# A linear-attention and MLP kernel: the weight loads are issued from ScalarE's queue after named steps, and each chunk's four input loads get staggered priorities

## The chip, the cores and the metric

The kernel runs on one core of one Trainium2 chip. The metric is device time in microseconds of one execution, as the median over repeated runs; lower is better. Before the change it is 200.94 us (three runs, 200.44 to 201.19).

## The reference

For 4 batches and 8 heads (sequence 768, head size 48, all float32) the reference runs a recurrence with a decay, lays the heads side by side, and sends the result through an MLP with a leaky ReLU:

```python
state = zeros(B, H, D, D)
for t in range(S):
    cur = einsum('bhd,bhe->bhde', u[None] * kt, vt)
    y[:, :, t] = einsum('bhd,bhde->bhe', rt, state + cur)
    state = wt[:, :, :, None] * state + einsum('bhd,bhe->bhde', kt, vt)
x = y.transpose(0, 2, 1, 3).reshape(B * S, H * D)      # 3072 x 384
h = x @ w_in                                           # 384 x 2048
out = maximum(0.01 * h, h) @ w_out                     # 2048 x 384
```

## The kernel before

**Chunks.** The 4 x 768 tokens are cut into 24 chunks of 128 tokens (`NCH`, six for each batch). A chunk needs four inputs, w, k, r and v, each a DMA of 192 KB in 192-byte rows: 128 tokens times 8 heads make 1024 rows (lines 288 to 295). The weights come in eight DMAs of 768 KB: four quarters of `w_in` in rows of 2048 bytes (384 rows each) and four of `w_out` in rows of 1536 bytes (512 rows each). Each quarter is cast to bf16 in two halves, one on DVE and one on ACT (lines 255 to 270).

**A chunk's preparation**, in the order in which one step needs the other: Ln of w on ACT (line 310); a cumulative sum on PE (325); the sum `ci` on DVE (340); two Exp on ACT, `er` (347) and `ek` (353); `rk`, which is r times `er` (360) and k times `ek` (366), on DVE; transposes on PE (379) with copies out on DVE (387) and ACT (389); scores on PE (450); the mask `m` on DVE (471); the sums for the state on PE (461) and the state on DVE (483, 485); the output product on PE (497, 501). On the side, POOL casts v to `vb` (316) and multiplies `ru` (406, 410), DVE reduces it to `dg` (414), and POOL makes `vs` from v and `dg` (418). DVE adds `y` (512), PE transposes it (521), and ACT copies it to `xT` (527). From chunk 16 on, the transposes are DMAs (397, 533).

**The MLP.** For each chunk there are four up steps (line 553: 12 matmuls each, quarter q of `w_in`), each followed by a leaky ReLU on ACT into `g` (587), and four down steps (line 605: 4 matmuls each, quarter q of `w_out`), then a copy on DVE (616) and the output DMA (620).

**The order of the work.** Nothing is scheduled on the chip: each engine, and each DMA queue with it, runs its instructions in the order in which they were written. That order comes from a list scheduler in the kernel, `Plan` (`order()`, from line 35). Each step is added with an engine, a planned duration, its dependencies and a priority. In planned time, a free engine takes the ready step with the lowest priority number, and among equals the one added first. A DMA step holds its queue for its planned duration; its planned transfer (`wire`) then waits for all transfers that were issued earlier, whatever the queue, and its data count as landed 1.5 us after that. The steps are emitted by planned start. Chunk n has priority P0 = 10n for its main steps, P0 + 1 for the scores, masks and outputs, and P0 + 2 for POOL's side work; the leaky ReLU has 5, the output copy 3, and the up and down steps have 1000 and more. Planned times decide only this order; on the chip each instruction waits for its semaphores.

**Buffers.** A `Ring` hands out a fixed set of tiles in turn, and whoever takes a tile again must wait for all earlier users of it. The ring `in` has 11 tiles, shared by chunk inputs and weights. The takes go: chunk 0 tile 0, chunk 1 tile 1, the `w_in` quarters tiles 2 to 5, chunk 2 tile 6, chunk 3 tile 7, the `w_out` quarters tiles 8, 9, 10 and 0, chunk 4 tile 1, chunk 5 tile 2, chunk 6 tile 3, and so on. So chunk 4 waits for the last reader of chunk 1, and chunks 5 and 6 wait for the casts of `w_in` quarters 0 and 1. The loads of chunk n also wait for the cumulative sum of chunk n - 5 (`AHEAD`), and the Ln of chunk n waits for the first up step of chunk n - 4 (`LEAD`). The cumulative sums, the scores and the outputs of a chunk each have a single PSUM tile, so the chunks pass these steps in order.

**Before the change** all loads are issued on SyncE's queue (SP), with the `w_in` quarters at priority 14, between chunks 1 and 2, and the `w_out` quarters at 34, between chunks 3 and 4. Their casts carry the same priorities.

Of the kernel before, what the change touches and what calls it, by code (L numbers as in the profile page):

```python
# [115 lines left out]
def kernel(  # L116
# [11 lines left out]
    nc = tc.nc  # L128
# [10 lines left out]
    NQ = FF // 512  # L139
# [1 line left out]
    LEAD = 4  # L141
    AHEAD = 5

    WEIGHTS = [(2, 14)] * 4 + [(4, 34)] * 4
    blocks = [1] * NCH
    assert sum(blocks) == NCH

# [41 lines left out]
    with tc.manual_schedule():  # L189
# [26 lines left out]
        def step(eng, dur, fn, pri, reads=(), writes=(), deps=(), wire=None):  # L216

            d = list(deps)
            for x in writes:
                d += x.old  # L220
            i = plan.add(eng, dur, fn, d, pri, wire)
            for x in (*reads, *writes):
                x.steps.append(i)
            return i
# [4 lines left out]
        def act(n, src=180):  # L229
            return (src + n) / 1200.0 + 0.02  # L230
# [4 lines left out]
        win_s, wout_s = [], []  # L235
        JQ = NJ // NQ

        def weight_steps(q, which, pri):
            st = in_r.take()

            def load(st=st, q=q):
                if which == 0:
                    nc.sync.dma_start(
                        out=st.t[:].rearrange("p (t f) -> p t f", t=KT),
                        in_=w_in_v[:, :, q * 512 : (q + 1) * 512],
                    )
                else:
                    nc.sync.dma_start(
                        out=st.t[:].rearrange("p (t f) -> p t f", t=JQ),
                        in_=w_out_v[:, q * JQ : (q + 1) * JQ, :],  # L250
                    )

            ld = step("SP", 0.45, load, pri, writes=[st], wire=2.2)
            made = []
            for half, eng in ((0, "DVE"), (1, "ACT")):
                def cast(st=st, q=q, half=half, eng=eng):
                    if which == 0:
                        f0 = half * 256
                        o = w_in_b[:, :, q * 512 + f0 : q * 512 + f0 + 256]
                        i = st.t[:].rearrange("p (t f) -> p t f", t=KT)[:, :, f0 : f0 + 256]  # L260
                    else:
                        n = JQ // 2
                        o = w_out_b[:, q * JQ + half * n : q * JQ + (half + 1) * n, :]
                        i = st.t[:].rearrange("p (t f) -> p t f", t=JQ)[:, half * n : (half + 1) * n, :]
                    if eng == "DVE":
                        nc.vector.tensor_copy(out=o, in_=i)
                    else:
                        nc.scalar.copy(out=o, in_=i)
                d = 0.65 if eng == "DVE" else act(768, 224)
                made.append(step(eng, d, cast, pri, reads=[st], deps=[ld]))  # L270
            (win_s if which == 0 else wout_s).append(made)


        xt_steps, cums, lns = [], [], []
        prev = None
        for n in range(NCH):
            b, c = divmod(n, C)
            t0 = c * L
            P0 = n * 10
            for i, (before, pri) in enumerate(WEIGHTS):  # L280
                if n == before:
                    weight_steps(i % NQ, i // NQ, pri)
            first, last = c == 0, c == C - 1
            slot = in_r.take()
            wn, kn, rn, vn = (
                View(slot, slot.t[:, i * DM : (i + 1) * DM].rearrange("p (h d) -> p h d", h=H)) for i in range(4))
            lds = []
            for src, use in ((w, wn), (k, kn), (r, rn), (v, vn)):
                def load(src=src, use=use, b=b, t0=t0):
                    nc.sync.dma_start(  # L290
                        out=use.t, in_=src[b, :, t0 : t0 + L, :].rearrange("h p d -> p h d")
                    )
                lds.append(step(
                    "SP", 0.45, load, P0, writes=[slot], wire=0.97,
                    deps=[cums[n - AHEAD]] if n >= AHEAD else []))
            if n == 0:
                u_ld = step(
# [4 lines left out]
                    P0, wire=0.6,  # L302
# [8 lines left out]
                P0, reads=[wn], writes=[lw], deps=[wl],  # L311
# [12 lines left out]
            def cum(cp=cp, lw=lw, tot=(not first and a_pe)):  # L324
# [18 lines left out]
                P0, reads=[cp, lw], writes=[ci], deps=[s_cum, s_ln],  # L343
# [5 lines left out]
                P0, reads=[cp], writes=[er], deps=[s_cum, s_ci],  # L349
# [5 lines left out]
                P0, reads=[ci], writes=[ek], deps=[s_ci],  # L355
# [6 lines left out]
                P0, reads=[rn, er], writes=[rk], deps=[rl, s_er],  # L362
# [5 lines left out]
                P0, reads=[kn, ek], writes=[rk], deps=[kl, s_ek],  # L368
# [25 lines left out]
            else:  # L394
# [4 lines left out]
                    P0, reads=[rk], writes=[rkT], deps=[s_r, s_k], wire=1.75)]  # L399
# [78 lines left out]
            if not last:  # L478
                sx = sx_r.take()
                s_st = []  # L480
                def state(sx=sx, pp=pp, sb=sb):
# [7 lines left out]
                    deps=[s_pp] + ([] if sb is None else s_sb)))  # L489
# [4 lines left out]
            def intra(m=m, vb=vb, yp=yp, rkT=rkT, sb=sb):  # L494
# [13 lines left out]
                deps=s_m + s_T + [s_vb] + ([] if sb is None else s_sb))  # L508
# [69 lines left out]
        for rank, (kind, nb, item) in enumerate(seq):  # L578
            pri = 1000 + rank
            if kind == 0:  # L580
                up, j, J, N, g, m_chs, deps = item
                hp = hp_r.take()
                s_up = step("PE", J * 3 * (N / 2400 + 0.0025), lambda up=up, hp=hp: up(hp), pri,
                            writes=[hp], deps=deps)
# [13 lines left out]
            else:  # L598
                ch, q, g, off = item
# [8 lines left out]
                deps = [g_done[nb, j] for j in range(q * NJ // 4, (q + 1) * NJ // 4)]  # L608
# [50 lines left out]
```

## Time and profile before

| | before |
|---|---|
| median of the runs | 200.94 us |
| the profiled execution | 199.18 us |
| its span, first to last instruction | 197.4 us |
| busy: PE, DVE, ACT, POOL | 175.4, 134.9, 113.7, 101.8 us |
| bytes moved on the one DMA queue of the kernel | 32.97 MB |

The profile is one execution. "Busy" counts the time in which an engine executes; for PE it is modelled, since matmuls overlap, so a busy PE is not always a PE at full rate. A row such as `29.60 1.53 SPq L290 ...` in a timeline gives start and duration of an instruction in microseconds from the start of the span, then its engine (SPq is SyncE's sequencer, which issues DMAs) and line. In the DMA view, the last number of a row is the median time from issue to landing.

### The profile page before, as it was taken

Reading aid. Unit: us, or ns where it says so; the run is one execution under the profiler, and the core shown is the slowest. Engines: PE = TensorE matmul, PEld = TensorE weight load, DVE = VectorE, ACT = ScalarE, POOL = GpSimd, SP = SyncE. Lnnn points to the kernel's source line nnn. Section 1 sums busy time; section 2 is a strip of 40 time slices with the busy share of each in tenths; the row PEclk is TensorE's granted clock in tenths of the full one; section 3 lists DMA queues with packets and bytes.
Section 4 is the critical chain, followed back from the end, with each engine's and each line's share of the span. In section 5 each row is a group of like instructions: output and inputs, shape, how many; then the busy total and the mean of one; then the engine's idle time right before and its main releaser. Section 6 shows DMA issues by size and latency. Waiting matters only on the chain.

```text
span 197.4 us, 5816 instructions
## 1 busy us (share of the span) xinstructions
PE 175.4 (89%) x2360; PEld 137.7 (70%) x2360; DVE 134.9 (68%) x223; ACT 113.7 (58%) x249; POOL 101.8 (52%) x126
## 2 busy tenths in 40 slices
PE   0426884999999999999999999999999989999992
PEld 0315773678777878767877788777778768778870
DVE  6578459856998989699988989647876665441111
ACT  3434795557785865846576765656565546434430
POOL 2483068245888997898698796571813110100000
PEclk9999998599999999999999999999999999999999
DMA  6999999989999999989999968989735729422002
GB/s 122 200 285 378 179 203 382 286 167 195 186 191 189 196 216 183 241 171 223 182 227 193 221 145 145 210 159 184 118 90 113 49 68 116 95 64 59 29 15 79
DMA packets 118954, 33.34 MB, mean 169 GB/s; under 512 B 112144, under 2 KB 117392, under 8 KB 118928
## 3 DMA queue, kind: packets, MB, share of 16 engines
q1 hardware_dynamic: 118928, 32.97, 82.6%
q8 instruction: 18, 0.29, 0.7%
q14 instruction: 8, 0.07, 0.1%
HBM read 25.36 MB, written 4.72 MB: 152 GB/s over the span
## 4 chain that ended last, share of the span: by engine, by line
PE 73%; DMA 8%; DVE 7%; ACT 5%; SPq 2%; issue 2%; POOL 1%; DVEq 0%; POOLq 0%
PE op L605 29%; PE hp L553 29%; PE sc L450 3%; PE sc L379 3%; DMA in<-in_r_dram 3%; DMA rkT<-rk 3%; DMA in<-in_v_dram 2%; PE yp L501 2%; SPq L290 2%; PE yp L461 2%; DVE m L471 2%; PE cp L325 2%; PE yp L497 1%; DVE rk L366 1%; DVE rk L360 1%
## 5 line engine op out<-in xcount | busy, mean ns | idle before, releaser
L587 ACT ACTIVATE g<-hp 128x512 bf16<-128x512 f32 x96 | 57.2, 598 | 47.7 <-PE hp L553 47.1
L553 PE MATMUL hp<-xT,w_in_b 128*128 128x128 bf16 x1152 | 81.8, 223 | 1.3 <-ACT xT L527 0.9
L553 PEld LDWEIGHTS <-w_in_b 128*128 128x128 bf16 x1152 | 71.9, 100 | 10.2 <-issue 1.0
L605 PE MATMUL op<-w_out_b,g 128*128 128x384 bf16 x384 | 78.3, 330 | 0.0
L605 PEld LDWEIGHTS <-g 128*128 128x128 bf16 x384 | 33.4, 98 | 14.2 <-issue 0.7
L406 POOL TENSOR_TENSOR ru<-in,ub 128x384 f32<-128x384 f32 x24 | 24.9, 1039 | 19.4 <-DMA in<-in_r_dram 18.6
L439 POOL TENSOR_TENSOR sb<-s,a 128x384 bf16<-128x384 f32 x20 | 19.6, 978 | 26.1 <-ACT a L432 16.6
L471 DVE TENSOR_TENSOR m<-sc,maskb 128x1024 bf16<-128x1024 f32 x24 | 29.2, 1219 | 5.3 <-PE sc L450 4.6
L616 DVE COPY o<-op 128x384 f32<-128x384 f32 x24 | 13.3, 552 | 18.3 <-PE op L605 18.3
L410 POOL TENSOR_TENSOR ru<-ru,in 128x384 f32<-128x384 f32 x24 | 25.4, 1056 | 0.4
L418 POOL TENSOR_TENSOR vs<-in,dg 128x384 f32<-128x384 f32 x24 | 20.7, 866 | 8.4 <-DVE dg L414 5.5
L366 DVE TENSOR_TENSOR rk<-in,ek 128x384 bf16<-128x384 f32 x24 | 20.5, 853 | 0.9 <-ACT ek L353 0.8
L360 DVE TENSOR_TENSOR rk<-in,er 128x384 bf16<-128x384 f32 x24 | 16.8, 701 | 5.4 <-ACT er L347 5.2
L340 DVE TENSOR_TENSOR ci<-cp,lw 128x384 f32<-128x384 f32 x24 | 13.2, 550 | 7.4 <-ACT g L587 4.0
L316 POOL CAST vb<-in 128x384 bf16<-128x384 f32 x24 | 13.2, 552 | 9.4 <-DMA in<-in_v_dram 7.2
L512 DVE TENSOR_TENSOR y<-yp,vs 128x384 bf16<-128x384 f32 x24 | 13.2, 550 | 7.0 <-PE yp L501 5.8
L347 ACT ACTIVATE er<-cp 128x384 f32<-128x384 f32 x24 | 11.9, 497 | 10.2 <-DVE ci L340 10.2
L379 PE MATMUL sc<-ident,rk 128*128 128x128 bf16 x128 | 13.2, 235 | 4.8 <-DVE rk L360 2.9
L389 ACT COPY rkT<-sc 128x512 bf16<-128x512 bf16 x16 | 9.4, 586 | 12.7 <-PE sc L379 6.7
L414 DVE TENSOR_REDUCE dg<-ru 128x8 f32<-128x384 f32 x24 | 13.0, 543 | 3.7 <-POOL ru L410 3.6
L379 PEld LDWEIGHTS <-rk 128*128 128x128 bf16 x128 | 8.8, 103 | 7.6 <-DVE rk L360 4.0
L310 ACT ACTIVATE lw<-in 128x384 bf16<-128x384 f32 x24 | 12.5, 520 | 2.1 <-DMA in<-in_w_dram 1.8
(39 smaller groups left out, 149.3 us busy)
## 6 DMA issues: line engine op xcount, KB each, us to landing
in<-in_w_dram SPq DMA_DIRECT2D x24, 192.0 KB, 4.3
in<-in_k_dram SPq DMA_DIRECT2D x24, 192.0 KB, 4.3
in<-in_r_dram SPq DMA_DIRECT2D x24, 192.0 KB, 4.8
in<-in_v_dram SPq DMA_DIRECT2D x24, 192.0 KB, 4.3
out_dram<-o SPq DMA_DIRECT2D x24, 192.0 KB, 2.6
in<-in_moe_w_in_dram SPq DMA_DIRECT2D x4, 768.0 KB, 7.9
in<-in_moe_w_out_dram SPq DMA_DIRECT2D x4, 768.0 KB, 8.3
ub<-in_u_dram SPq DMA_DIRECT2D x1, 192.0 KB, 4.6
```

What stands on the lines that cost most here:

```text
L360: lambda rk=rk, rn=rn, er=er: nc.vector.tensor_tensor(out=rk.t[:, 0, :, 0:D], in0=rn.t, in1=er.t[:], op=ALU.mult),
L366: lambda rk=rk, kn=kn, ek=ek: nc.vector.tensor_tensor(out=rk.t[:, 1, :, 0:D], in0=kn.t, in1=ek.t[:], op=ALU.mult),
L379: nc.tensor.transpose(trv[:, a, g, :], rk.t[:, a, 2 * g : 2 * g + 2, :].rearrange("p h d -> p (h d)"), ident[:])
L406: lambda ru=ru, rn=rn: nc.gpsimd.tensor_tensor(out=ru.t[:], in0=rn.t, in1=ubv, op=ALU.mult),
L410: lambda ru=ru, kn=kn: nc.gpsimd.tensor_tensor(out=ru.t[:], in0=ru.t[:], in1=kn.t, op=ALU.mult),
L418: lambda vs=vs, vn=vn, dg=dg: nc.gpsimd.tensor_tensor(out=vs.t[:], in0=vn.t, in1=dg.t[:].unsqueeze(2).to_broadcast([128, H, D]), op=ALU.mult),
L439: lambda sb=sb, s_in=s_in, a_in=a_in: nc.gpsimd.tensor_tensor(out=sb.t[:].rearrange("p g a d -> p (g a) d"), in0=s_in.t[:].rearrange("p g ...
L471: lambda m=m, sc=sc: nc.vector.tensor_tensor(out=m.t[:].rearrange("p a g t -> p (a g) t"), in0=sc.t[:].rearrange("p a g t -> p (a g) t"), ...
L553: nc.tensor.matmul(hp.t[:, a * N : (a + 1) * N], lhsT=w_in_b[:, t, (j + a) * 128 : (j + a + 1) * 128], rhs=xT[:, t, c0 : c0 + N], start=(a ...
L587: lambda hp=hp, g=g, j=j, J=J, N=N: nc.scalar.activation(out=g.t[:, j : j + J, 0:N], in_=hp.t[:, 0 : J * N].rearrange("p (a n) -> p a n", ...
L605: nc.tensor.matmul(op.t[:], lhsT=g.t[:, j, off : off + 128], rhs=w_out_b[:, j, :], start=(j == 0), stop=(j == NJ - 1))
L616: "DVE", dve(DM, 120), lambda o=o, op=op: nc.vector.tensor_copy(out=o.t[:], in_=op.t[:]),
```

## The change

The eight weight loads move from SyncE's queue to ScalarE's. Each now depends on one Ln step, chunk 0's for `w_in` and chunk 2's for `w_out` (the third number of each `WEIGHTS` entry), and the priorities of loads and casts go from 14 to 2 and from 34 to 3. The planner is told 0.1 us on ACT for an issue in place of 0.45 us on SP, a transfer of 2.0 us in place of 2.2, and 0.95 in place of 0.97 for an input load. The four input loads of a chunk get priorities P0, P0 + 0.1, P0 + 0.2 and P0 + 0.3; the load of `u`, which was added after them, keeps P0 of chunk 0.

```diff
-    WEIGHTS = [(2, 14)] * 4 + [(4, 34)] * 4
+    WEIGHTS = [(2, 2, 0)] * 4 + [(4, 3, 2)] * 4
...
-        def weight_steps(q, which, pri):
+        def weight_steps(q, which, pri, after):
...
-                    nc.sync.dma_start(
+                    nc.scalar.dma_start(
                         out=st.t[:].rearrange("p (t f) -> p t f", t=KT),
                         in_=w_in_v[:, :, q * 512 : (q + 1) * 512],
                     )
                 else:
-                    nc.sync.dma_start(
+                    nc.scalar.dma_start(
                         out=st.t[:].rearrange("p (t f) -> p t f", t=JQ),
                         in_=w_out_v[:, q * JQ : (q + 1) * JQ, :],
                     )
 
-            ld = step("SP", 0.45, load, pri, writes=[st], wire=2.2)
+            ld = step("ACT", 0.1, load, pri, writes=[st], deps=[lns[after]], wire=2.0)
...
-            for i, (before, pri) in enumerate(WEIGHTS):
+            for i, (before, pri, after) in enumerate(WEIGHTS):
                 if n == before:
-                    weight_steps(i % NQ, i // NQ, pri)
+                    weight_steps(i % NQ, i // NQ, pri, after)
...
-            for src, use in ((w, wn), (k, kn), (r, rn), (v, vn)):
+            for i, (src, use) in enumerate(((w, wn), (k, kn), (r, rn), (v, vn))):
...
                 lds.append(step(
-                    "SP", 0.45, load, P0, writes=[slot], wire=0.97,
+                    "SP", 0.45, load, P0 + 0.1 * i, writes=[slot], wire=0.95,
                     deps=[cums[n - AHEAD]] if n >= AHEAD else []))
```

## The prediction

> **What bounds the kernel now.** I read the page first: the busy shares, then the slices.
>
> ```profile
> span 197.4 us, 5816 instructions
> ...
> PE   0426884999999999999999999999999989999992
> ...
> PEclk9999998599999999999999999999999999999999
> DMA  6999999989999999989999968989735729422002
> GB/s 122 200 285 378 179 203 382 286 167 195 186 191 189 196 216 183 241 171 223 182 227 193 221 145 145 210 159 184 118 90 113 49 68 116 95 64 59 29 15 79
> ```
>
> A slice is 4.9 us. From slice 7 (35 us, the slices counted from 0) PE is full to the end; before it there are holes, and slices 6 and 7 have a lower granted clock. The DMA engines are full from slice 1 to about slice 20, at some 190 GB/s, and at 380 GB/s where weights pass. So the first 35 to 40 us are a DMA stage, and everything after them is a queue of PE work. Next I read the windows, over all engines, then for the down and the up matmuls alone.
>
> ```profile
> 15.00:20.00 5.00, 3.43 (x34) 2.79 (x35) 4.36 (x7) 2.15 (x3) 1.37 (x2) 1.00 1.03 377
> 35.00:40.00 5.00, 5.00 (x37) 3.13 (x36) 4.24 (x8) 2.53 (x4) 1.07 (x1) 0.52 1.04 264
> 60.00:65.00 5.00, 4.93 (x76) 4.10 (x75) 4.43 (x8) 3.05 (x9) 4.45 (x7) 1.00 0.94 208
> 53.00:193.70 140.70, 139.15 (x1935) 109.63 (x1931) 97.81 (x161) 83.53 (x187) 76.17 (x88) 1.00 0.78 147
> ...
> 0.00:53.00 53.00, 10.09 (x44) 4.21 (x44) 0.94 1.01 235
> ...
> 0.00:53.00 53.00, 14.52 (x187) 13.18 (x188) 0.94 1.01 235
> ```
>
> From 53.0 to PE's last work at 193.7 us PE idles 140.70 - 139.15 = 1.55 us. So the span is set by how much matmul work is done by some early time, say 53 us, when before has done 44 down matmuls (first short row) and 187 up matmuls (last row). Their rates, at full clock, are in the chain of waits, with two pieces of a chunk's preparation:
>
> ```profile
> 40.17 0.65 PE op L605 x4
> ...
> 45.56 0.67 PE hp L553 x12
> ...
> 65.86 0.22 PE sc L379 x4
> ...
> 67.57 0.33 PE sc L450 x8
> ```
>
> A down matmul is 0.65 / 4 = 0.163 us, an up matmul 0.67 / 12 = 0.056 us.
>
> **Part 1: the order on SP changes by more than the weights that leave it.** This decides my forecast, and it comes out of the planner's rules with the code's own costs, worked by hand (an order is taken from them, no time). In the changed plan, chunk 0's w lands at 0.45 + 0.95 + 1.5 = 2.9, its Ln is done at 3.5, and the `w_in` issues follow at once on ACT. Eight input or `u` transfers are queued ahead of them (to 7.70), so quarters 0 and 1 land at 11.2 and 13.2; v of chunk 1, issued between quarters 1 and 2, lands at 14.15. The casts now have priority 2 instead of 14, so they pass chunk 1's steps: quarter 0 is cast by 12.7 and quarter 1 by 14.1. That frees tiles 2 and 3, which are those of chunks 5 and 6. Tile 1, for chunk 4, waits for chunk 1's `vs`, which needs that v and a `dg` at about 15.0: done at about 15.9. So SP is given chunks 2, 3, **5, 6, 4**. In the old plan `vs` and the late cast come at 15.2 and 15.5, and chunk 4 goes first. My margins are 3.2 us for chunk 5 and 1.8 for chunk 6, against an error by hand of perhaps 1.
>
> The `w_out` issues wait for chunk 2's Ln, at about 21 in the plan. By then the transfers of chunks 2, 3, 5, 6 and 4 are queued (to 35.65), so the plan has `w_out` landing from 39.15, but chunk 4's w at 34.3 and r at 36.2. So Ln, cumulative sum, Exp and the transposes of chunk 4 are written ahead of the `w_out` casts on ACT and DVE, and ahead of the first down step on PE. Whatever the chip does with `w_out`, no down matmul starts until chunk 4's r has landed and been worked on.
>
> **Part 2: when that is.** SP's timeline, and four answers of the DMA view for the issues at 29.60, 40.55, 44.22 and 46.32:
>
> ```profile
> 26.47 3.04 SPq L248 DMA_DIRECT2D in<-in_moe_w_out_dram  x4
> 29.60 1.53 SPq L290 DMA_DIRECT2D in<-in_w_dram  x1
> ...
> 40.55 0.73 SPq L290 DMA_DIRECT2D in<-in_w_dram  x1
> ...
> 44.22 1.06 SPq L290 DMA_DIRECT2D in<-in_w_dram  x1
> ...
> 46.32 0.98 SPq L290 DMA_DIRECT2D in<-in_r_dram  x1
> ```
> ```profile
> in<-in_w_dram SPq DMA_DIRECT2D x1, 192.0 KB, 11.2
> ...
> in<-in_w_dram SPq DMA_DIRECT2D x1, 192.0 KB, 4.1
> ...
> in<-in_w_dram SPq DMA_DIRECT2D x1, 192.0 KB, 4.5
> ...
> in<-in_r_dram SPq DMA_DIRECT2D x1, 192.0 KB, 5.0
> ```
>
> The w of chunks 4, 5 and 6 lands at 40.8, 44.7 and 48.7, one load a microsecond. In the new order chunk 4 comes where chunk 6 is now: w at 48.7, r at 46.32 + 5.0 = 51.3. That holds if the engines' total work ahead of it is unchanged, in whatever order the queues share it: the DMA share is 0.94 where only inputs pass and 1.03 where only weights do, so there is no free room for one beside the other. The Trainium skill, "DMA: Bandwidth & Descriptors", section "Issuing engines are not separate DMA queues", speaks against the change in the same sense: DMAs from SyncE and ScalarE interleave on the same 16 engines, and a second issuer saves issue time only. Both shares agree with it.
>
> From r on the path goes over DVE: `rk`, twice, then the copy of the transposes and the first cast. The groups:
>
> ```profile
> L366 DVE TENSOR_TENSOR rk<-in,ek 128x384 bf16<-128x384 f32 x24 | 20.5, 853 | 0.9 <-ACT ek L353 0.8
> ...
> L360 DVE TENSOR_TENSOR rk<-in,er 128x384 bf16<-128x384 f32 x24 | 16.8, 701 | 5.4 <-ACT er L347 5.2
> ```
> ```profile
> 35.07 1.44 PE L605 MATMUL op<-w_out_b,g 128*128 128x384 bf16 x4
> ```
>
> 51.3 + 0.70 + 0.85 makes 52.85, and the first down step comes at about 53, where it starts at 35.07 now. Bounds: 51.3 if the cast needs nothing behind r, and 54.5 if it stands behind chunk 4's `dg`. I take 53, as the `w_out` step becomes ready in the plan between the two.
>
> **Part 3: the sum.** At 53 us the changed kernel has done all 192 up matmuls of chunks 0 to 3 and no down matmul. It lacks 44 x 0.163 = 7.2 us, has 5 x 0.056 = 0.3 us more, and is behind by part of a chunk's preparation: with eight transposes (2 x 0.22), eight scores (0.33) and as much again for the rest, a chunk takes about 1.6 us; half of one, 0.8 us. Together 7.7 us. PE has little to do before 53 us, so it may restart at a low clock: the row at 35.00 shows 0.52 over 5 us, a loss of 2.4 us, which before has already paid within its 53 us. Between 0 and 2.4 I take 1.2. Of the 1.55 us of later idling, waits for inputs should go, since PE comes later than they do: 0 to 1.55 back, I take 1.0. The sum is 7.7 + 1.2 - 1.0 = **+7.9 us**: 207.1 us against the profiled execution's own 199.18 (197.4 of span and 1.8 around it), and 208.8 us against the median of 200.94.
>
> **Part 4: what is hidden.** The `u` load overtakes k, r and v of chunk 0, since it keeps P0 and they no longer do; it holds SP 0.93 us. And the four `w_in` issues stand on ACT between chunk 0's Ln and `er`:
>
> ```profile
> 3.54 0.93 SPq L299 DMA_DIRECT2D ub<-in_u_dram  x1
> ...
> 8.67 3.10 SPq L243 DMA_DIRECT2D in<-in_moe_w_in_dram  x4
> ...
> 3.93 0.52 ACT L310 ACTIVATE lw<-in 128x384 bf16<-128x384 f32 x1 [1.85 <-DMA in<-in_w_dram]
> 5.61 0.49 ACT L347 ACTIVATE er<-cp 128x384 f32<-128x384 f32 x1 [1.16 <-DVE ci L340]
> ```
>
> No DMA is issued on ACT now. Four issues took SP 3.10 us; ACT may take between nothing and that. From 4.45 the issues end at 7.55 at most, so `er` moves by up to 1.9 us, beside the wait for r. The other four (3.04 us on SP) block ACT after chunk 2's Ln, with copies of transposes and leaky ReLUs behind them; the fourth also waits for the readers of chunk 0, long done. I cost both at nothing, as the down steps wait for chunk 4 until 53 anyway; without that cover they cost 2 to 5 us. The 6.1 us that SP no longer spends on weights give nothing back: its issues are held up by the full queue (0.7 to 1.5 us each above).
>
> **The rivals.** *The queues add up (faster).* If the 190 GB/s is a limit of SP's queue and not of the engines, weights pass beside inputs. The weights take about 17 us of the shared line (8 x 0.79 MB at 377 GB/s), so chunk 4's w lands at 48.7 - 17 = 31.7, 9 us sooner than now. PE's holes in slices 3 to 6 come to 4.9 x (0.4 + 0.2 + 0.2 + 0.6) = 6.9 us and the low clock to 2.4; of these 9 us some 6 would be filled: 195 us. It decides from where chunk 4's w lands by about 41, as it does now. For it: 190 against 380 GB/s. Against: both shares at 1. Chance 0.13. *The order of the chunks stays 4, 5, 6.* If my hand plan errs by over 2 us, chunk 4 lands as now, the weights a few us sooner, and PE fills part of the same holes with down steps, until it runs out of chunks: some 2 us, 199 us, chance 0.12. *It does nothing:* the same bytes, the same PE work, gains and losses cancel within half a percent (1.0 us, about what can be told from no change here); 201 us, chance 0.07. *Weights crowd out the first chunks (slower still).* If the engines alternate row by row between the queues, four `w_in` quarters (4 x 384 rows) let only 1536 input rows pass, 1.5 loads, over some 10 us from about 6.5. Chunk 0's v then lands near 14, chunk 1's w near 17; in the plan chunk 1's Ln stands on ACT ahead of a copy of chunk 0 (7.3 against 7.8), so everything up to the first up step moves to about 21.6, and chunk 3's up steps (4 x 0.67 = 2.7 us) slip behind 53: 211.6 us, chance 0.18. The first up step shows today at:
>
> ```profile
> 18.60 1.46 PE L553 MATMUL hp<-xT,w_in_b 128*128 128x128 bf16 x12 [0.39 <-DVE w_in_b L266]
> ```
>
> The Trainium skill's same page, "Queues, rings and completion order", says that each engine goes round its queues packet by packet, which is this rival's mechanism; with one queue in use, no run here shows it yet.
>
> **How the numbers follow.** My forecast has 0.50: 208.8, with 205 to 212 of its own from the bounds (first down step 51.3 to 54.5, clock 0 to 2.4, idling 0 to 1.55). Slower by over 0.5% are the forecast and the crowding, 0.68; within 0.5% the last but one, 0.07; faster the first two rivals, 0.25. The range runs from 197.5, which leaves out the queues that add up (0.13), to 214, which leaves out the end of the crowding.
>
> **What would show it.** Right: SP's chunk loads in the order 2, 3, 5, 6, 4; chunk 4's w landing near 48 and r near 51; the first down step on line 605 near 53, with `w_out` landed well before; PE in holes until then and full after. A DMA share near 1 and a sum of rates no better than 380 GB/s while both queues are active. Wrong: chunk 4's loads ahead of 5 and 6, a first down step before 45, or 192-byte loads landing at one a microsecond while weights pass.

## The result and the profile after

The changed kernel takes 220.46 us (three runs, 219.96 to 222.07) against 200.94 before: 1.0995 times as long, with a 95% interval of 1.09 to 1.1089. Some executions of a kernel run slower than the rest, and a ratio with an interval is taken over the fast ones alone, so it need not be the quotient of the two medians. The forecast was 208.8 with a range up to 214. The direction was right; of the 19.5 us that were lost, the forecast had 7.9.

The page of the changed kernel, span and slices (5.5 us each):

```profile
span 218.3 us, 5803 instructions
...
PE   0004872085998999999999999999999999999993
...
PEclk9999969655599999999999999999999999999998
DMA  5999999999994399894794687599894432521111
GB/s 124 327 266 257 187 172 250 293 288 188 179 192 63 93 187 214 184 194 94 130 181 96 125 146 156 102 201 176 154 162 104 103 89 48 123 57 54 39 38 72
```

PE does next to nothing in the first three slices, and in slices 6 and 7 (33 to 44 us) it has a hole that the kernel before does not have. It is full from slice 10 (55 us), not from 35 us. The DMA engines are full up to slice 11 and then short of work for two slices; they were never slack while PE waited. The granted clock is low in slice 5 and in slices 7 to 10, ahead of the hole, in it and behind it.

Next the windows with all engines: the changed kernel from 65.5 us to PE's last work, then the same for the kernel before.

```profile
65.50:214.30 148.80, 147.18 (x2003) 114.58 (x2000) 105.94 (x168) 88.92 (x197) 78.17 (x89) 1.00 0.61 123
```
```profile
65.50:193.70 128.20, 126.71 (x1756) 99.68 (x1753) 86.03 (x142) 74.63 (x168) 65.37 (x76) 1.00 0.75 142
```

From 65.5 us on PE is full in both: 1.62 and 1.49 us idle. The changed kernel simply has 147.18 - 126.71 = 20.5 us more PE work left at that moment, and its span is 20.9 us longer. So the loss lies wholly ahead of 65.5 us. For the down matmuls (line 605) alone, then the up matmuls (553), the same view of the changed kernel has:

```profile
0.00:65.50 65.50, 0.00 (x0) 0.02 (x1) 0.82 1.10 227
...
0.00:65.50 65.50, 17.48 (x192) 16.08 (x192) 0.82 1.10 227
```

This is the state that the prediction foresaw, 192 up and no down matmuls, but 12.5 us later than the 53 us it gave. PE's timeline shows the two places (start, duration, and in brackets the idle time ahead and who ended it):

```profile
23.94 1.44 PE L553 MATMUL hp<-xT,w_in_b 128*128 128x128 bf16 x12 [0.57 <-ACT xT L527]
...
44.22 2.72 PE L553 MATMUL hp<-xT,w_in_b 128*128 128x128 bf16 x24 [9.84 <-ACT g L587]
...
65.53 1.46 PE L605 MATMUL op<-w_out_b,g 128*128 128x384 bf16 x8
```

The first up step comes at 23.9 us (before, 18.6), and PE then waits 9.84 us for a leaky ReLU of ScalarE. ScalarE's timeline says why:

```profile
3.71 11.61 ACTq L243 DMA_DIRECT2D in<-in_moe_w_in_dram  x4
...
15.37 0.49 ACT L347 ACTIVATE er<-cp 128x384 f32<-128x384 f32 x1 [11.15 <-DMA in<-in_v_dram]
...
32.75 10.78 ACTq L248 DMA_DIRECT2D in<-in_moe_w_out_dram  x4
...
43.57 0.60 ACT L587 ACTIVATE g<-hp 128x512 bf16<-128x512 f32 x1 [10.23 <-DMA in<-in_v_dram]
```

ScalarE stands still twice, 11.6 and 10.8 us, while it issues four DMAs each time, and the timeline puts both waits down to the landing of a chunk's v. Neither `er` nor `g` reads a v. Seen in narrower windows, the issues themselves are short; the third and the fourth of each set are late:

```profile
6.62 0.44 ACTq L243 DMA_DIRECT2D in<-in_moe_w_in_dram  x1
...
14.95 0.38 ACTq L243 DMA_DIRECT2D in<-in_moe_w_in_dram  x1
...
40.15 0.37 ACTq L248 DMA_DIRECT2D in<-in_moe_w_out_dram  x1
...
43.15 0.38 ACTq L248 DMA_DIRECT2D in<-in_moe_w_out_dram  x1
```

And the chain that ended last has these pieces, the two DMA rows being its longest of all:

```profile
3.02 11.91 DMA in<-in_v_dram
14.93 0.02 issue
14.95 0.38 ACTq L243
...
33.78 9.27 DMA in<-in_v_dram
43.07 0.04 ACTq L248
43.11 0.04 issue
43.15 0.38 ACTq L248
```

The fourth `w_in` issue starts at 14.95, when v of chunk 0 has landed (3.02 + 11.91 = 14.93); the fourth `w_out` issue at 43.15, when v of chunk 6 has (43.05). These are loads of SyncE, into other tiles. The compiled program has the link: every DMA of SyncE and of ScalarE signals one of eight semaphores, dealt in turn in the order in which the DMAs stand in the program, and waits, before it is issued, for the last DMA that had its semaphore, which is the eighth before it. Eight before the fourth `w_in` load stands v of chunk 0; eight before the fourth `w_out` load, v of chunk 6. The third issues agree: eight before them stand k of chunk 0 and k of chunk 6, which were issued at 1.92 and 32.18 and landed 4.7 and 7.9 us later, and the third issues start at 6.62 and 40.15. As long as SyncE issued everything, only SyncE waited there. On ScalarE the same wait holds up whatever is written behind it: Exps, leaky ReLUs, copies. DMAs of GpSimd have semaphores of their own and carry no such wait.

### The profile page after: what moved, and what is told of

It is laid out like the page before. It is cut to its first block, busy times and chain, and to the rows that moved or that the text cites. A ratio compares the mean times of both kernels' runs of the same rounds, so it can differ in the third digit from the quotient of the medians.

```text
span 218.3 us, 5803 instructions
## 1 busy us (share of the span) xinstructions
PE 178.2 (82%) x2360; PEld 141.0 (65%) x2360; DVE 136.9 (63%) x223; ACT 114.6 (52%) x249; POOL 102.0 (47%) x126
## 4 chain that ended last, share of the span: by engine, by line
PE 63%; DMA 14%; DVE 11%; issue 5%; ACT 3%; SPq 2%; ACTq 0%; DVEq 0%
PE hp L553 26%; PE op L605 23%; DMA in<-in_v_dram 10%; DMA rkT<-rk 5%; PE sc L379 4%; PE sc L450 3%; DVE m L471 2%; DVE rk L360 2%; PE yp L461 2%; DVE rkT L387 1%; SPq L290 1%; PE yp L501 1%; ACT rkT L389 1%; PE cp L325 1%; DVE rk L366 1%
## 5 line engine op out<-in xcount | busy, mean ns | idle before, releaser
L553 PE MATMUL hp<-xT,w_in_b 128*128 128x128 bf16 x1152 | 84.4, 227 | 11.4 <-ACT g L587 9.8
L553 PEld LDWEIGHTS <-w_in_b 128*128 128x128 bf16 x1152 | 74.2, 102 | 18.8 <-issue 10.5
L605 PE MATMUL op<-w_out_b,g 128*128 128x384 bf16 x384 | 77.0, 326 | 1.0 <-DVE w_out_b L266 1.0
L439 POOL TENSOR_TENSOR sb<-s,a 128x384 bf16<-128x384 f32 x20 | 18.2, 910 | 28.2 <-ACT a L432 20.8
L410 POOL TENSOR_TENSOR ru<-ru,in 128x384 f32<-128x384 f32 x24 | 26.1, 1087 | 0.4
L379 PE MATMUL sc<-ident,rk 128*128 128x128 bf16 x128 | 13.5, 241 | 13.8 <-DVE rk L360 12.6
L316 POOL CAST vb<-in 128x384 bf16<-128x384 f32 x24 | 14.4, 601 | 6.9 <-DMA in<-in_v_dram 6.9
L310 ACT ACTIVATE lw<-in 128x384 bf16<-128x384 f32 x24 | 12.4, 518 | 1.7 <-DMA in<-in_w_dram 1.6
```

The lines of the kernel that those rows point to most:

```text
L316: lambda vb=vb, vn=vn: nc.gpsimd.tensor_copy(out=vb.t[:], in_=vn.t),
L379: nc.tensor.transpose(trv[:, a, g, :], rk.t[:, a, 2 * g : 2 * g + 2, :].rearrange("p h d -> p (h d)"), ident[:])
L410: lambda ru=ru, kn=kn: nc.gpsimd.tensor_tensor(out=ru.t[:], in0=ru.t[:], in1=kn.t, op=ALU.mult),
L439: lambda sb=sb, s_in=s_in, a_in=a_in: nc.gpsimd.tensor_tensor(out=sb.t[:].rearrange("p g a d -> p (g a) d"), in0=s_in.t[:].rearrange("p g ...
L553: nc.tensor.matmul(hp.t[:, a * N : (a + 1) * N], lhsT=w_in_b[:, t, (j + a) * 128 : (j + a + 1) * 128], rhs=xT[:, t, c0 : c0 + N], start=(a ...
L605: nc.tensor.matmul(op.t[:], lhsT=g.t[:, j, off : off + 128], rhs=w_out_b[:, j, :], start=(j == 0), stop=(j == NJ - 1))
```

## The experiments

The theory: the loss has three parts, the planned order (as all on one queue would show it), the crowding of the chunk inputs by weights on a second queue, and ScalarE's second stop. Rivals: the late chunk 4 alone, the crowding alone, or the first stop. Where nothing else is said a time is one run, beside a run of the kernel before at 199.3 to 201.0. Seventeen runs of the kernel before spread from 198.05 to 202.31; of their pairs one in six differs by over 2 us and one in seventeen by over 3 us, so a difference under 3 us between two single runs is not taken for one. The versions are explained one by one below; "act" in a name is ScalarE. "Stops" are the stretches from the first to the last of ScalarE's four `w_in` and four `w_out` issues, in us.

| version | us | first up step | first down step | stops |
|---|---|---|---|---|
| after | 220.46 | 23.94 | 65.53 | 11.6, 10.8 |
| win_act_wout_gpsimd | 209.61 | 23.98 | 54.88 | 11.7, none |
| win_gpsimd_wout_act | 220.69 | 24.46 | 66.28 | none, 12.4 |
| same_plan_on_gpsimd | 209.81 | 23.57 | 55.33 | none |
| same_plan_on_sync | 204.96 | 15.73 | 46.87 | none |
| only_win_on_act | 209.86 | 24.38 | 55.45 | 12.1, none |
| only_wout_on_act | 210.46 | 15.45 | 55.80 | none, 3.4 |
| fewer_dmas | 216.72 | 22.75 | 61.89 | 0.4, none |
| win_at_start | 216.56 | 28.74 | 52.83 | 9.6, 11.8 |
| chunks_in_order | 214.32 | 23.78 | 54.15 | 11.5, 6.3 |
| four_first | 221.79 | 24.03 | 67.18 | 11.7, 12.3 |
| four_first_gpsimd | 209.38 | 23.18 | 54.36 | none |
| four_first_sync | 203.12 | 15.61 | 47.23 | none |

**Each stop taken away by itself.** Each of these two moves one set of weights to GpSimd's queue, so that both sets still pass on another queue than the inputs, with the same plan.

```diff
 # win_act_wout_gpsimd: only the w_out issue
-                    nc.scalar.dma_start(
+                    nc.gpsimd.dma_start(
                         out=st.t[:].rearrange("p (t f) -> p t f", t=JQ),
```

> The changed kernel with one edit: the w_out quarters are issued on GpSimd's queue, where they wait for no earlier load, in place of ScalarE's; w_in stays on ScalarE. Theory (of the 19.5 us, about 10 are the second stop of ScalarE, at the w_out issues, where the leaky ReLU of the up steps waits behind them; its first stop costs next to nothing of its own): the first stop of 11 to 12 us stays, the first up step stays at 23 to 25 us, there is no stop of ScalarE and no hole of 8 us or more in PE between 34 and 44 us, and the time is 207 to 213 us. Rival (what costs the 10 us is that both sets of weights share the bandwidth with the inputs at these times, whichever engine issues them, or both stops together): 217 to 222 us.

> The mirror image: w_in on GpSimd's queue, w_out on ScalarE's as in the changed kernel. Theory (the second stop alone is worth about 10 us): er of chunk 0 is back at 5.6 us, the first up step still comes at 23 to 24 us (crowding by w_in), ScalarE still stops for 6 to 11 us at the w_out issues with a hole in PE behind it, and the time is 215 to 221 us. Rival (the first stop carries the loss, by what it delays later): 208 to 212 us.

The mirror image makes the same edit on the `w_in` issue. Measured were 209.61 and 220.69. ScalarE and PE with `w_in` on ScalarE and `w_out` on GpSimd:

```profile
3.67 11.69 ACTq L243 DMA_DIRECT2D in<-in_moe_w_in_dram  x4
...
15.41 0.49 ACT L347 ACTIVATE er<-cp 128x384 f32<-128x384 f32 x1 [11.23 <-DMA in<-in_v_dram]
...
23.98 1.44 PE L553 MATMUL hp<-xT,w_in_b 128*128 128x128 bf16 x12 [0.57 <-ACT xT L527]
...
54.88 1.46 PE L605 MATMUL op<-w_out_b,g 128*128 128x384 bf16 x8
```

The first stop is there in full and costs nothing that can be seen: 209.61 against 209.81 with no stop at all, and a first up step at 23.98 against 23.57. The mirror image:

```profile
5.61 0.49 ACT L347 ACTIVATE er<-cp 128x384 f32<-128x384 f32 x1 [1.26 <-DVE ci L340]
...
33.53 11.88 ACTq L248 DMA_DIRECT2D in<-in_moe_w_out_dram  x3
45.46 0.60 ACT L587 ACTIVATE g<-hp 128x512 bf16<-128x512 f32 x1 [11.58 <-DMA in<-in_w_dram]
...
46.11 2.72 PE L553 MATMUL hp<-xT,w_in_b 128*128 128x128 bf16 x24 [11.33 <-ACT g L587]
```

`er` of chunk 0 is back at 5.6 us, the second stop and PE's hole behind it stay, and so does the whole loss. The second stop alone is worth 220.46 - 209.61 = 10.9 us. The edit that takes it away also issues `w_out` 4 to 11 us earlier, but that is not what PE waited for: in the changed kernel the last `w_out` quarter, issued at 43.15, landed 6.5 us later, 16 us ahead of the first down step, and the wait of 9.84 us was for a leaky ReLU. Both times came out as the theory said; the stop of the mirror image, 12.4 us from the first issue on, was longer than the 6 to 11 expected.

**All weights on one other engine.** The changed plan word for word, with all eight weight loads issued by GpSimd, or by SyncE.

```diff
-                    nc.scalar.dma_start(
+                    nc.gpsimd.dma_start(
...
-                    nc.scalar.dma_start(
+                    nc.gpsimd.dma_start(
```

> The changed kernel with the same plan, but the eight weight DMAs are issued from GpSimd's queue. The transfers still run beside the inputs; the chunks still come in the order 5, 6, 4; only ACT has no DMA to issue. 'ACT is held': the Exp of chunk 0 starts at 6 to 8 us instead of 15.4, no hole of PE beyond 5 us after the first up step, first down step near 53, time 207 to 211. Rival 'crowding' (weights beside inputs starve chunk 0, whoever issues them): v of chunk 0 still lands near 15, the first up step stays near 24, time 215 or more.

> The changed kernel with the same plan and the same order of instructions, but the eight weight DMAs are issued from SyncE's queue, as before. No second queue, no issue on ACT; the chunks still come in the order 5, 6, 4, and the w_out quarters stand behind chunk 4 on SP. 'ACT is held': 205 to 210 us, since only the order is left. 'Order' says the same, 207 to 209. 'Crowding' the same. If it stays near 220, all three fall, and the planned order itself is the cost.

209.81 and 204.96, both beside 201.0 for the kernel before. On SyncE the planned order is left without a second queue: it costs 4.0 us, and the first down step comes at 46.87. Here `w_out` is issued behind chunk 4's v, as the plan has it. GpSimd adds a second queue, without waits, and 4.85 us. So the first range holds, and 204.96 lies just under the second. Of the marks of crowding the late first up step came (23.57), but v of chunk 0 landed at 7.9 and not near 15; the weights were issued later here (4.87 for 3.71). Chunk 1's w came late instead, and its Ln stands on ScalarE ahead of a copy of chunk 0 (first row). GpSimd's timeline (the other rows) shows that an issue took longer there than on ScalarE, some 0.8 us, without harm:

```profile
16.25 0.52 ACT L310 ACTIVATE lw<-in 128x384 bf16<-128x384 f32 x1 [9.73 <-DMA in<-in_w_dram]
```
```profile
4.87 3.21 POOL L243 DMA_DIRECT2D in<-in_moe_w_in_dram  x4
...
28.16 3.04 POOL L248 DMA_DIRECT2D in<-in_moe_w_out_dram  x4
```

**One set on ScalarE, the other on SyncE.**

```diff
 # only_win_on_act: the w_out issue; only_wout_on_act: the w_in issue
-                    nc.scalar.dma_start(
+                    nc.sync.dma_start(
```

> The w_in quarters stay on ScalarE's queue, the w_out quarters go back to SyncE's, with the same plan otherwise. Theory (the second stop of ScalarE, at the w_out issues, is worth about 10 us, and the crowding of chunk 0's v by w_in about 5): the first stop of ScalarE stays (about 11 us before er of chunk 0), the first up step stays at 23 to 24 us, there is no stop of ScalarE near 33 us, and the time is 207 to 213 us. Rival (the two stops are worth little, the time goes with the weights' share of the bandwidth and with the late w_out): 217 to 222 us.

> The w_in quarters go back to SyncE's queue, the w_out quarters stay on ScalarE's, with the same plan otherwise. Theory: the first up step comes at 15 to 17 us, as with all weights on SyncE; ScalarE still stops at the w_out issues, for less than 10.8 us, since the loads that the third and fourth issue wait for (r of chunk 2 and w of chunk 3) land earlier here; the time is 200 to 208 us. Rival (two queues crowd each other at any stage): chunk 4 lands past 45 us as after the change, and the time is 212 us or more.

With `w_in` alone 209.86, inside the theory's range. With `w_out` alone 210.46, and this falsified part of it: the stop was short as expected (3.4 us with all four issues), the first up step early (15.45), yet the time lay above 208. The rival's mark was met, chunk 4's r landing past 45 us (at 50.0), though not its 212 us. ScalarE's timeline, then the windows:

```profile
23.88 2.97 ACTq L248 DMA_DIRECT2D in<-in_moe_w_out_dram  x3
...
39.77 0.52 ACT L310 ACTIVATE lw<-in 128x384 bf16<-128x384 f32 x1 [8.13 <-DMA in<-in_w_dram]
```
```profile
25.00:30.00 5.00, 2.00 (x30) 1.58 (x27) 1.64 (x4) 3.05 (x8) 2.37 (x4) 1.00 0.99 331
30.00:35.00 5.00, 2.02 (x33) 1.60 (x33) 2.73 (x5) 1.24 (x3) 0.83 (x1) 0.82 1.10 335
```

From 25 to 35 us 331 and 335 GB/s pass, where inputs alone had some 190 in the kernel before, and a w of 192 KB is waited for until 39.8 us. So `w_out` crowds the inputs too. The parts do not add up: on its own each set costs some 5 us beside the inputs (209.86 and 210.46 against 204.96), and both together without the second stop cost no more (209.61). Why they do not is not shown.

**Fewer DMAs.** `w_in` in one DMA, `w_out` in two. The later quarters of `w_in` lie in tiles that chunk loads overwrite ahead of their casts, so the up steps compute with other weights than the reference's; the work is the same.

```diff
-    in_r = ring("in", 11, [128, 1536], F32)
+    in_big = pool.tile([128, 11 * 1536], F32, name="in_big")
+    in_r = Ring([in_big[:, i * 1536 : (i + 1) * 1536] for i in range(11)])
...
+                    if q:
+                        return
...
-                        out=st.t[:].rearrange("p (t f) -> p t f", t=KT),
-                        in_=w_in_v[:, :, q * 512 : (q + 1) * 512],
+                        out=in_big[:, 2 * 1536 : 6 * 1536].rearrange("p (t f) -> p t f", t=KT),
+                        in_=w_in_v,
```

> The changed kernel with the same plan and the same bytes on ScalarE's queue, but w_in comes in one DMA (384 rows of 8192 bytes) and w_out in two (three quarters, then one). In the program the one w_in DMA has fewer than eight DMAs before it. Theory 'ACT is held by the eighth DMA before': the first stop of ACT (11.6 us) vanishes, chunk 0's Exp starts at 6 to 8 us, the second stop is at most some 6 us; time 208 to 214. Rival 'ACT is held by the transfer': an issue returns only as the queue takes the rows, whatever their number, so ACT stands for 8 us or more at the one w_in DMA, and the time stays at 217 or more.

Both stops vanished: the issues took 0.41, 0.37 and 0.43 us, and `er` of chunk 0 came at 5.61. The time, 216.72, lies outside the theory's range and just under the rival's. PE waits once for 7.05 us for a cast of `w_in`, and this cast, on DVE at 30.92, had waited for a chunk's k, which is loaded over a quarter that is not yet cast. For `w_in`, with fewer than eight DMAs ahead of it, this shows that the stop goes with the number of DMAs in the program and not with the bytes. The `w_out` issues also came later (39.38 for 32.75), so for the second stop it shows less, and of what a stop is worth it tells nothing.

**Other places for the issues and the loads.** `win_at_start` issues `w_in` without waiting for the first Ln; `chunks_in_order` makes the loads of chunk n, from 5 on, wait in the plan for the landing of chunk n - 1.

```diff
 # win_at_start
-            ld = step("ACT", 0.1, load, pri, writes=[st], deps=[lns[after]], wire=2.0)
+            ld = step("ACT", 0.1, load, pri, writes=[st], deps=[lns[after]] if which else [], wire=2.0)
 # chunks_in_order
-                    deps=[cums[n - AHEAD]] if n >= AHEAD else []))
+                    deps=([cums[n - AHEAD]] if n >= AHEAD else []) + ([prev_ld] if n >= 5 else [])))
```

> The changed kernel, but the four w_in issues do not wait in the plan for chunk 0's Ln: they stand first on ACT. 'ACT is held', with its cause that a weight issue waits until the eighth DMA before it in the program has landed: the first two go at once, the third waits for chunk 0's w (about 4 us) and the fourth for its k, so that the first stop shrinks from 11.6 us to 4 to 7; the second stop stays near 10; time 212 to 217. 'Crowding': weights start 3 us earlier, chunk 0's inputs come later still, and the time is 220 or more.

> The changed kernel, but the loads of chunk n (from 5 on) stand behind those of chunk n - 1 in the plan, so that SP issues chunk 4 before 5 and 6 and the first down steps are planned some 8 us earlier. Theory 'ACT is held': most of the extra 20 us comes from the two stops of ACT, in which it stands at weight issues for 11.6 and 10.8 us. Both stops stay here, PE keeps a hole of 8 us or more behind the second, and the time stays at 212 to 218. Rival 'order' (the prediction): the order 5, 6, 4 is the cost, and with it gone the time falls to 205 or less.

216.56 and 214.32, both within the expected times, but not all the marks came. In `win_at_start` the first stop shrank to 9.6 us and not to 4 to 7, since chunk 0's w and k came later beside the weights (6.4 and 10.0 us), and the second is 11.8 us, 9.9 of them without a break. In `chunks_in_order` the second stop is 6.3 us and PE's hole behind it 4.62 and not 8 or more. That hole, PE's wait behind the second stop, goes with the time. Here it is for `chunks_in_order`, `win_at_start` and, from below, `four_first` (the number in brackets):

```profile
40.00 2.72 PE L554 MATMUL hp<-xT,w_in_b 128*128 128x128 bf16 x24 [4.62 <-ACT g L588]
```
```profile
38.44 0.61 PE L450 MATMUL sc<-rkT 48*128 48x128 bf16 x8 [6.95 <-ACT rkT L389]
```
```profile
46.66 2.72 PE L555 MATMUL hp<-xT,w_in_b 128*128 128x128 bf16 x24 [11.05 <-ACT g L589]
```

With holes of 4.62, 6.95, 9.84 (the changed kernel), 11.05 and 11.33 us (the mirror image) the times lie 4.7, 7.0, 10.9, 12.2 and 11.1 us above the 209.61 of the version without a second stop. These are single runs, and other things move in them too (the first up step is at 28.74 in `win_at_start`, the order of all later loads is another in `chunks_in_order`), but the five agree within 1.2 us: the second stop cost about as long as PE waited behind it, and its own length (6.3 to 12.4 us) goes with the time less well.

**Chunk 4 ahead of 5 and 6.** The prediction let everything hang on this order. In the plan, the loads of chunks 5 and 6 also wait for the readers of chunk 4's tile; on ScalarE's, GpSimd's and SyncE's queue.

```diff
+            if n == 4:
+                held = list(slot.old)
...
-                    deps=[cums[n - AHEAD]] if n >= AHEAD else []))
+                    deps=([cums[n - AHEAD]] if n >= AHEAD else []) + (held if n in (5, 6) else [])))
```

> The changed kernel, with chunks 5 and 6 made ready in the plan no earlier than chunk 4, so that SP's order is 4, 5, 6 again; nothing waits for a landing. 'ACT is held': both stops stay, time 213 to 217. 'Order': 205 or less; if the two add up, 214.

> As four_first, with the weight DMAs issued from GpSimd's queue: no order 5, 6, 4, nothing held on ACT, only weights beside inputs. If the three causes add up (20 us = about 10 for ACT held, 4 to 6 for the order, 5 for crowding), this one keeps the crowding alone: 204 to 207. If crowding costs nothing by itself, 201 or less.

> All on SyncE's queue with the changed plan (that was 204.96 us), but chunk 4 is issued ahead of chunks 5 and 6. Theory (the order 5, 6, 4 by itself costs nothing; the 4 us are those of w_out, which is issued behind all three chunks): 204 to 206 us, first down step at 45 to 48 us. Rival (the late chunk 4 is the 4 us): 200 to 202 us.

221.79 against 220.46, 209.38 against 209.81, 203.12 against 204.96: nothing that can be told from no change. My ranges for the first two, 213 to 217 and 204 to 207, were missed, as I had put 4 to 6 us on the order; the 203.12 lies between the ranges of theory and rival. So no cost of the order of these chunks can be told, and the largest difference is 1.8 us. The chain of waits of the version on GpSimd shows what came in its place:

```profile
30.22 13.47 DMA in<-in_w_dram
...
43.78 0.52 ACT lw L312
44.33 0.59 ACT rkT L391
```

Chunk 4's w is now issued at 26.0, ahead of the `w_out` loads, and the late load is the next one, chunk 5's: issued at 30.2, when `w_out` passes, it lands 13.5 us later. Its Ln stands on ScalarE ahead of a copy of chunk 3's transposes and of the `w_out` casts. Here another order only made another chunk late.

**A version that is a little faster than before.** All loads stay on SyncE's queue at their old priorities; only the casts get the priorities 2 and 3, and chunk 4 keeps its place by the edit above.

```diff
 # on the kernel before
-                made.append(step(eng, d, cast, pri, reads=[st], deps=[ld]))
+                made.append(step(eng, d, cast, 2 + which, reads=[st], deps=[ld]))
```

> The kernel before, all on SyncE, with the casts' priorities 2 and 3 as in the change and chunk 4 kept ahead of 5 and 6. This asks whether the one useful thing in the change, casts that don't wait behind chunk 1, is a gain by itself: first up step near 16 instead of 18.6; time 197 to 200 if PE can use it, 201 if chunk 4's arrival near 41 sets the pace anyway.

> The kernel before, with all loads on SyncE's queue at their old priorities, where only the priorities of the casts go to 2 and 3 and chunk 4 keeps its place ahead of chunks 5 and 6. One look gave 198.81 against 199.99 us. Theory (earlier casts bring the first up step from 18.6 to 16.5 us, and nothing else moves): faster by 0.3 to 1.0%. Rival (the earlier up steps only move work): the same time within 0.3%.

A single run gave 198.81. Over 12 runs the median is 197.83, against 200.27 over 17 runs of the kernel before; the ratio is 0.9917 (95% interval 0.9881 to 0.9954), so it is 0.8% faster, a small gain inside the theory's range. The two edits were not taken apart. Its first up step:

```profile
16.25 1.46 PE L555 MATMUL hp<-xT,w_in_b 128*128 128x128 bf16 x12 [0.85 <-DVE w_in_b L266]
```

This is 2.4 us sooner than the 18.60 before. That the gain in time comes from there is likely and not shown.

## Why the prediction was right or wrong

**What bounds the kernel: right.** PE's work left at a given moment sets the end; 20.5 us more of it made 20.9 us of span.

**Part 1, the order on SP: right as an order, wrong as the cause.** SP was given chunks 2, 3, 5, 6, 4. But with chunk 4 first again the time stays (the three runs above), so "this decides my forecast" was not so. What the plan as a whole costs on one queue is 4.0 us (204.96 against 201.0, one run each), and chunk 4 first took 1.8 of that back in one run, which is not told from none. That the rest is `w_out` being issued behind the chunks (first down step at 46.87 for 35.07) is argued and not shown.

**Part 2: landing right, the step behind it wrong.** Chunk 4's w was put at 48.7 and its r at 51.3. SP's timeline, and the DMA view's answers for these two issues (last number: issue to landing):

```profile
35.93 4.78 SPq L290 DMA_DIRECT2D in<-in_w_dram  x1
...
42.01 2.34 SPq L290 DMA_DIRECT2D in<-in_r_dram  x1
```
```profile
in<-in_w_dram SPq DMA_DIRECT2D x1, 192.0 KB, 10.4
...
in<-in_r_dram SPq DMA_DIRECT2D x1, 192.0 KB, 8.5
```

They landed at 46.3 and 50.5. The first down step followed 1.7 us after r in the prediction, and 15 us after it on the chip: at 50.5 us chunk 3's `er` had only just been computed, chunk 2's having waited until 44.06 behind ScalarE's stop. I followed chunk 4's own chain and took the chunks ahead of it, which pass the same PSUM tiles in order, as done.

**Part 3, the sum: near without the stop, with one term of the wrong sign.** With the second stop gone and all else as changed, the first down step comes at 54.9 (I had 53, bounds 51.3 to 54.5) and the time is 209.6 (208.8). Here are two windows of that version, the second from 53 us to PE's last work:

```profile
40.00:50.00 10.00, 8.66 (x99) 0.56 1.08 200
53.00:204.28 151.28, 148.68 (x2025) 1.00 0.70 136
```

PE's work left at 53 us is 148.68 - 139.15 = 9.5 us more than before, where I had put 7.7 + 1.2 = 8.9. The clock cost more than the 2.4 us that I took as its bound: at 0.56, 8.66 us of work lose up to 3.8 (an estimate, 8.66 x 0.44). The later idling is 2.6 us in place of 1.55, so 1.0 us more and not 1.0 less as I took it. Together that is 10.5 us, the difference of the two profiled spans (207.9 and 197.4); against the median of 200.94 its one run is 8.7 us longer. That the forecast of 7.9 comes out close is partly chance, since the version without the stop has the crowding in it too, at 4.65 us above the plan on one queue, which I had as a rival and not as a part of the forecast.

**Part 4, the ScalarE issues at nothing: this step failed.** "I cost both at nothing", with 3 us as the bound of one set of issues and 2 to 5 without the cover. I priced the issues by what SP spends on four of them, 3.10 us, and looked for a wait only in the tiles that they write. The issues took 0.4 us each; the wait in front of them took 10.8 us. The cover failed too: the down steps do wait for chunk 4, but chunk 4 waits in order for chunks 2 and 3, and these stood behind the stop. From version to version: 4.0 us for the plan on one queue, 4.65 for the second queue, 10.85 for the second stop. They are differences of one run to the next, so they add up to the 19.5 by construction; the 10.85 is the one that other runs bear out.

**The rivals.** The crowding of the first chunks came, as a part and not as an alternative: v of chunk 0 landed at 14.93 (I had 14) and the first up step came at 23.9 (21.6). With no stop of ScalarE it came as late (23.57), there by chunk 1's w, which landed at 16.2 (I had 17). This rival's time adds 2.7 to 208.8, which is 211.5 and not 211.6. The queues do not add up: over the first 65.5 us 227 GB/s passed (shown above), against 228 in the kernel before, and the two queues together reach at most 327 GB/s in a slice, under the 382 that one queue reached before. The Trainium skill's rule of the prediction, "DMA: Bandwidth & Descriptors", section "Issuing engines are not separate DMA queues", that a second issuer saves issue time only, agrees with this; that the issuer itself then stood still for 10.8 us is not in that rule.

## What to carry to other kernels

Before a DMA goes to an engine that also computes, list from the compiled program what its issue waits for, the completion semaphore that it shares with earlier DMAs included, and then what is written behind it on that engine. A wait that costs nothing on a queue which only issues DMAs can cost its full length in front of an Exp or a leaky ReLU, as the second stop did, or nothing, as the first did, where PE had to wait for late inputs anyway. And a second queue does not only share the bandwidth, it chooses anew who is served first: small rows that had the engines to themselves now take turns with large ones, and get few bytes for a turn.

## What the runs showed of the hardware

With two queues full, the DMA engines served them row by row in some stretches and not in others. The profile counts each row as a packet (and under 20 short ones besides, in each row below); q1 is SyncE's queue with rows of 192 bytes, q10 ScalarE's with the weights. The first number of a row is the packets. First `only_wout_on_act` from 30 to 34 us, then the changed kernel from 7.3 to 9.6 us:

```profile
q10 hardware_dynamic: 798, 1.20, 90.6%
q1 hardware_dynamic: 795, 0.15, 19.6%
```
```profile
q10 hardware_dynamic: 427, 0.84, 101.6%
q1 hardware_dynamic: 52, 0.01, 2.1%
```

In the first stretch 798 packets of the weights, in rows of 1536 bytes, went by for 795 of the inputs, which so had an eighth of the bytes. In the second it was 52 for 427, and no run here shows why. Either way the small rows lose: r of chunk 0 landed at 7.3 and v, the next load on its queue, at 14.9, so a load that takes 1 us where only inputs pass took 7.6. The Trainium skill, "DMA: Bandwidth & Descriptors", section "Queues, rings and completion order", has the engines go round their queues packet by packet. The 798 to 795 agree with that at one row for a turn, the 427 to 52 do not.

An issue on ScalarE took 0.37 to 0.51 us, one on GpSimd 0.76 to 0.80 on average (four in 3.04 and 3.21 us). I had not expected the wait for the eighth DMA before, and it belongs to the program and not to the chip: 11.6 us of it cost no time in the end, and 10.8 us cost all of their length.
